# Transposing queries and keys of a head together on all 128 rows, in a fused attention and gated-FFN kernel

## The chip, the core and the metric

The kernel runs on one core of one Trainium2 chip. A core has a matrix engine (TensorE, "PE" in the profile, with its weight loads listed apart as "PEld"), a vector engine (VectorE, DVE), an activation engine (ScalarE, ACT), a general engine (GpSimd, POOL) and a queue engine (SyncE, SP); 16 DMA engines move data between HBM and the on-chip memory. TensorE writes to PSUM banks, which the other engines empty. The metric is the device time of one execution in microseconds (us).

## The reference

The inputs are q, k and v with 8 batches, 12 heads, 448 positions and 64 elements a head, and the three weights of a gated FFN (768 to 1536 and back to 768). Types are float32 outside; the kernel computes in bfloat16 with float32 sums.

```
scores = q k^T / sqrt(64)
attn   = max(scores, 0)^2 / 448
x      = attn v, heads side by side: 3584 rows of 768
out    = (gelu(x w_gate) * (x w_val)) w_out
```

There is no softmax, so no row sums are needed: each block of scores can be activated and squared by itself.

## The kernel before

**Layout.** A batch has 448 = 64 x 7 positions; position p*7 + c lies on partition p in chunk c. `qk16[b]` holds a batch's queries on partitions 0 to 63 and its keys on partitions 64 to 127. All other matmuls are cut into tiles of 64 rows by 64 columns, four of which lie beside each other in the array: two row halves (lists PE0, "lower", and PE1, "upper") and two column halves.

**Stages of a batch.** The scores need q and k with the head dimension on the partitions, so each batch's q and k are first transposed into `qkT`. A pair of heads is the unit: `NPAIR` is 6, and `NM` = 3 groups `m` of two pairs `r` each. For batches 0 and 1 (`EARLY` = 2) TensorE does it (`add_transposes`, the matmuls of line 333) and DVE copies the result out of PSUM (line 339). For later batches `add_dma_transposes` regroups the loaded data on DVE (line 258) and SP issues DMA transposes (line 262). Then come 21 score units a batch (`add_scores`, each with a relu on ScalarE, line 387, and a square on DVE, line 393), the values (`add_values`, copied to `xT` on line 443), gate and value matmuls for 12 blocks `fc` (`add_gate_value`: gelu on line 482, product on line 487), and the output matmuls (`add_out`). Batch b+1's attention runs interleaved with batch b's FFN.

**Transposes before.** For a group the kernel makes 56 matmuls: for both row halves i (0 = q, 1 = k), each pair r, each chunk c and each head j of the pair, a 64x64 block of `qk16` is the stationary operand and the identity moves. Each of the two halves i gathers both pairs in a PSUM area of its own, and its copy writes 64-element pieces into `qkT`. For batch 0 these areas are buffers of `psF` (`FB` = 4, handed out by `new_bank`), for batch 1 the two halves of one buffer of `psS` (`SB` = 2, shared with the scores). Batch 0's first group is handled pair by pair, `rs` = (0,) and then (1,).

**The order.** Nothing is left to a compiler: the schedule is written out by a small planner, `run_plan`. PE0 is a fixed list, sorted by a due time `at` that the loop at the end (lines 610 to 628) gives each step; PE1 follows PE0's positions (`both`: beside it, `then`: after its last). POOL is fixed too, in the order of the load calls on lines 561 to 587. The operations of ACT, DVE, SP and a pseudo-engine IDLE are taken from pools by earliest planned start. An operation is written into the program at the moment it is planned, and each engine executes in that order. `IDLE` operations emit nothing; they stand for the wait on loads ahead of a regrouping copy. Where the plan leaves TensorE idle, `fill` inserts dummy matmuls of `warm` (line 296) as long as the planned time is below `FILL`; `emit_warm_up` (line 676) puts 20 at the start.

**Loads.** POOL issues all loads. q and k of batch 0 come in pieces of heads 0-2, 2-4, 4-8 and 8-12; the FFN's weights follow between batch 1's pieces. Loads of batch b+2 are issued behind products of batch b (lines 500 to 508).

Of the kernel before, what the change touches and what calls it, by code (L numbers as in the profile page):

```python
# [88 lines left out]
def kernel(  # L89
# [10 lines left out]
    nc = tc.nc  # L100
# [6 lines left out]
    P = 64  # L107
# [13 lines left out]
    WOG = 3  # L121
    SB = 2
    FB = 4
    FILL = 64.0
    EARLY = 2

    out_scale = 1.0 / (D * S)
# [110 lines left out]
    def qkT_tile(b):  # L238
        if b not in qkT:
            qkT[b] = tpool.tile([128, NM * SC * 2, 2 * P], bf16, name="qkT", tag="qkT")  # L240
        return qkT[b]

    def by_group(t):
        return t.rearrange("d (m c r) x -> d m c r x", m=NM, c=SC)
# [3 lines left out]
    def add_dma_transposes(b, m):  # L248


        wait = Op("IDLE", 2.0, lambda: None,
                  [head_op[b, pr, i] for pr in (2 * m, 2 * m + 1) for i in range(2)])
        IDLE.append(wait)

        def emit_copy():
            if b not in qkr:
                qkr[b] = lpool.tile([128, NM, SC, 4, D], bf16, name="qkr", tag="qkr")
            nc.vector.tensor_copy(  # L258
                qkr[b][:, m], qk16[b].rearrange("p (h c d) -> p c h d", c=SC, d=D)[:, :, 4 * m:4 * m + 4])

        def emit_transpose(c0, c1):
            nc.sync.dma_start_transpose(
                by_group(qkT_tile(b))[:, m, c0:c1].rearrange("d c r x -> d (c r) x"),
                qkr[b][:, m, c0:c1].rearrange("p c h d -> p (c h d)"))

        copy = Op("DVE", 0.65, emit_copy, [wait, *tr_op.get((b - 1, m), ())], lag=0.15, prio=3)
        DVE.append(copy)
        tr_op[b, m] = [Op("SP", 0.19 * 2 * (c1 - c0), lambda c0=c0, c1=c1: emit_transpose(c0, c1),
                          [copy, last_s.get(b - 2)], lag=4.5) for c0, c1 in ((0, VC), (VC, SC))]
        SP.extend(tr_op[b, m])  # L270
# [9 lines left out]
    def new_bank(reader, shape=(128, 512), dtype=f32):  # L280
        in_bank.append(reader)
        return psF.tile(list(shape), dtype, name="ff", tag="F")

    def fill(t0, t1):

        reader = in_bank[-FB] if len(in_bank) >= FB else None
        if reader is not None:
            if reader.end is None:
                return
            t0 = max(t0, reader.end + 0.2)  # L290
        n = int((t1 - t0 - 0.15) / 0.115)
        if t1 > FILL or n < 1:
            return
        t = new_bank(None)
        for _ in range(n):
            nc.tensor.matmul(t[:, 0:256], warm[:, 0:128], warm[:, 0:256], start=True, stop=True)  # L296

    def ring_dep():
        return [ring[-FB]] if len(ring) >= FB else []
# [19 lines left out]
    def add_transposes(at, b, m, rs):  # L319

        box = {}

        def emit(i, n, c):
            if b and not box:
                t = psS.tile([128, 2, 1024], bf16, name="sp", tag="S")
                for x in range(2):
                    box[x] = t[:, x, 0:len(rs) * SC * P].rearrange("d (r x) -> d r x", r=len(rs))
            elif i not in box:
                box[i] = new_bank(t_op[b, m, rs[0], i], [128, len(rs), SC * P], bf16)
            t = box[i]  # L330
            src = qk16[b].rearrange("p (h c d) -> p h c d", c=SC, d=D)
            for j in range(2):
                nc.tensor.transpose(  # L333
                    t[HALF[j], n, c * P:(c + 1) * P], src[HALF[i], 2 * (2 * m + rs[n]) + j, c, :],
                    ident[HALF[i], HALF[i]], tile_position=(P * i, P * j))

        def emit_copy(i):
            dst = by_group(qkT_tile(b))[:, m].rearrange("d c r x -> d r c x")
            nc.vector.tensor_copy(  # L339
                dst[:, rs[0]:rs[-1] + 1, :, HALF[i]],  # L340
                box[i].rearrange("d r (c p) -> d r c p", c=SC))

        ops = [[], []]
        for i in range(2):
            have = [*(head_op[b, 2 * m + r, i] for r in rs), *(units[-SB:1 - SB] if b else ring_dep())]
            for n in range(len(rs)):
                for c in range(SC):
                    ops[i].append(Op(f"PE{i}", 0.05, lambda i=i, n=n, c=c: emit(i, n, c),
                                     have, lag=0.2))
            t = Op("DVE", 0.07 + 0.235 * len(rs), lambda i=i: emit_copy(i),  # L350
                   [ops[i][-1], last_s.get(b - 2)], lag=0.2, prio=1)
            for r in rs:
                t_op[b, m, r, i] = t
            DVE.append(t)
            if not b:
                ring.append(t)
        if b:
            units.append(t)
        both(at, zip(*ops), GS / 2 if b else 0.0)

    def add_scores(at, b, u):


        m, w = divmod(u, SC)
        tail = w == VC - 1
        prs = (2 * m, 2 * m + 1) if tail else (2 * m + (w > VC - 1),)
        cl = w if w < VC else w - VC
        box = {}

        def emit(j, pr):  # L370
            if not box:
                box[0] = psS.tile([128, 2, 512], f32, name="sp", tag="S")
            sp = box[0]
            t = by_group(qkT_tile(b))[HALF[j], m, :, pr % 2, :]
            for i in range(2):
                if tail:
                    n0 = (pr % 2) * S // 2
                    qs = t[:, :, i * P // 2:(i + 1) * P // 2]
                    mm(sp[HALF[i], j, n0:n0 + S // 2].rearrange("k (c p) -> k c p", c=SC),
                       t[:, VC - 1, HALF[1]], qs, j, i, True, True)  # L380
                else:
                    mm(sp[HALF[i], j, 0:S].rearrange("k (c p) -> k c p", c=SC),
                       t[:, cl + i * VC, HALF[1]], t[:, :, HALF[0]], j, i, True, True)

        def emit_relu():
            rl = box[1] = rpool.tile([128, 2, S], bf16, name="rl", tag="rl")
            nc.scalar.activation(rl[:, :, :], box[0][:, :, 0:S], AF.Relu)  # L387

        def emit_sq():
            a = apool.tile([128, 2, S], bf16, name="attnT", tag="attnT")  # L390
            for pr in prs:
                att[b, pr, VC - 1 if tail else cl] = a
            nc.vector.tensor_tensor(a[:, :, :], box[1][:, :, :], box[1][:, :, :], op=ALU.mult)  # L393

        if b < EARLY:
            have = [t_op[b, m, pr % 2, i] for pr in prs for i in range(2)]
        else:
            have = tr_op[b, m]
        have = [*have, *units[-SB:1 - SB]]
        ops = [[Op(f"PE{j}", 0.095 if tail else 0.189, lambda j=j, pr=pr: emit(j, pr), have, lag=0.24)  # L400
                for pr in prs] for j in range(2)]
        last_s[b] = ops[1][-1]
        relu = Op("ACT", 0.8, emit_relu, [ops[0][-1], ops[1][-1], *sq_list[-4:-3]], lag=0.18, prio=2)
        n_a = len(sq_list)
        sq = Op("DVE", 0.54, emit_sq, [relu, *att_free[n_a - 12:n_a - 11]] if n_a >= 12 else [relu],
                lag=0.2, prio=2)
        units.append(relu)
        sq_list.append(sq)
        att_free.append(None)
        for pr in prs:  # L410
            sq_op.setdefault((b, pr), []).append((sq, n_a))
            sq_of[b, pr, VC - 1 if tail else cl] = sq
        ACT.append(relu)
        DVE.append(sq)
        both(at, zip(*ops))
# [194 lines left out]
    for b in range(B):  # L610
        if b == 0:
            lo, hi = -60.0, -12.0
        elif b == 1:
            lo, hi = LO1, starts[1] - LEAD
        elif b == 2:
            lo, hi = starts[1] + 6.0, starts[2] - LEAD
        else:
            lo, hi = starts[b - 1] - LEAD, starts[b] - LEAD
        step = (hi - lo) / NU
        if b < EARLY:  # L620
            for m in range(NM):
                for rs in ((0,), (1,)) if b == m == 0 else ((0, 1),):
                    work.append((lo + SC * m * step - (5.0 if b else 3.0), 1, add_transposes, (b, m, rs)))
        for pr in range(NPAIR):
            u = SC * (pr // 2) + (VC - 1, SC - 1)[pr % 2]
            work.append((lo + u * step + max(4.5, (3.2 if b == 0 else 2.5) * step), 2, add_values, (b, pr)))
        for u in range(NU):
            work.append((lo + u * step, 3, add_scores, (b, u)))
# [83 lines left out]
```

## Time and profile before

| | us |
|---|---|
| median of 4 runs | 432.11 |
| lowest and highest | 431.10 and 433.21 |
| the profiled execution | 431.10 |
| its span in the profile | 429.3 |

The span runs from the first to the last instruction on the core; 1.8 us of the profiled execution's time lie around it. The second part of the page cuts the span into 40 slices of 10.7 us; each digit is the busy share in tenths.

```
PE   8989799999999999999999999999999999999995
DVE  3966565377544674366623675346633555212200
ACT  3956564276665655555455565555546555222221
DMA  7999999999334895269923798259913100220024
```

Transposes of line 333 fall into the first five slices (5.6 to 53.7 us); the dummy matmuls of line 296 run from 6.1 to 28.6 us. In the profile's groups by line a name such as `qkT<-ff` says what is written from what; `sp` is a buffer of `psS`, `ff` one of `psF`. In a time line the columns are start, length, engine, line, operation, names and count; in brackets stands how long the engine was idle before it and what released it, where "issue" means that the profile shows nothing it waited for.

| group | count | mean ns |
|---|---|---|
| transposes, line 333, matmuls | 336 | 192 to 201 |
| their weight loads | 336 | 112 |
| DVE copy of 896 elements to `qkT`, line 339 | 10 | 620 to 623 |
| DVE copy of 448 elements to `qkT`, line 339 | 4 | 389 |
| regrouping copy, line 258 | 18 | 1080 |
| relu of a score unit, line 387 | 168 | 920 |
| square of a score unit, line 393 | 168 | 623 |

Matmul lengths include their latency; matmuls overlap, so the mean is not what one costs in a row of many.

### The profile page before, as it was taken

Reading aid. Unit: us, or ns where it says so; the run is one execution under the profiler, and the core shown is the slowest. Engines: PE = TensorE matmul, PEld = TensorE weight load, DVE = VectorE, ACT = ScalarE, POOL = GpSimd, SP = SyncE. Lnnn points to the kernel's source line nnn. Section 1 sums busy time; section 2 is a strip of 40 time slices with the busy share of each in tenths; the row PEclk is TensorE's granted clock in tenths of the full one; section 3 lists DMA queues with packets and bytes.
Section 4 is the critical chain, followed back from the end, with each engine's and each line's share of the span. In section 5 each row is a group of like instructions: output and inputs, shape, how many; then the busy total and the mean of one; then the engine's idle time right before and its main releaser. Section 6 shows DMA issues by size and latency. Waiting matters only on the chain.

```text
span 429.3 us, 19964 instructions
## 1 busy us (share of the span) xinstructions
PE 418.5 (97%) x9279; PEld 365.1 (85%) x9279; DVE 212.2 (49%) x345; ACT 224.6 (52%) x323; POOL 71.6 (17%) x117
## 2 busy tenths in 40 slices
PE   8989799999999999999999999999999999999995
PEld 4668599778998888979999978979999978977895
DVE  3966565377544674366623675346633555212200
ACT  3956564276665655555455565555546555222221
POOL 8655420123000230023100230012200000000000
PEclk9999999999999999999999999999999999999998
DMA  7999999999334895269923798259913100220024
GB/s 106 197 199 198 201 208 183 165 148 164 59 76 96 86 173 60 76 105 148 122 52 101 91 157 93 76 81 145 147 40 77 40 4 2 52 64 3 3 76 111
DMA packets 75378, 44.92 MB, mean 105 GB/s; under 512 B 36128, under 2 KB 71840, under 8 KB 75296
## 3 DMA queue, kind: packets, MB, share of 16 engines
q0 software_dynamic: 37088, 24.39, 43.1%
q1 hardware_dynamic: 37968, 19.08, 26.1%
q8 instruction: 72, 1.18, 1.1%
q10 hardware_dynamic: 240, 0.20, 0.2%
q14 instruction: 10, 0.08, 0.1%
HBM read 48.76 MB, written 11.01 MB: 139 GB/s over the span
## 4 chain that ended last, share of the span: by engine, by line
PE 94%; DVE 3%; ACT 1%; issue 1%; ACTq 0%
PE ff L159 84%; PE sp L159 7%; DVE attnT L393 1%; PE ff L676 1%; ACT rl L387 1%; DVE qkT L339 1%; PE ff L296 1%; PE sp L333 1%; DVE xT L443 0%; PE ff L333 0%; ACT osb L538 0%; ACTq L543 0%; DVE warm L145 0%; ACTq L387 0%; ACTq L538 0%
## 5 line engine op out<-in xcount | busy, mean ns | idle before, releaser
L159 PE MATMUL ff<-xT,wg 64*64 64x448 bf16 x2304 | 219.4, 349 | 2.2 <-issue 2.2
L159 PE MATMUL ff<-xT,wv 64*64 64x448 bf16 x2304 | 218.4, 349 | 0.0
L387 ACT ACTIVATE rl<-sp 128x896 bf16<-128x896 f32 x168 | 152.1, 920 | 101.6 <-PE sp L159 81.3
L159 PE MATMUL ff<-wo,uT 64*64 64x384 bf16 (+1 forms) x2736 | 150.7, 320 | 0.5 <-issue 0.5
L159 PEld LDWEIGHTS <-wg 64*64 64x64 bf16 x2304 | 127.1, 107 | 17.4 <-issue 3.5
L393 DVE TENSOR_TENSOR attnT<-rl 128x896 bf16<-128x896 bf16 x168 | 104.0, 623 | 74.9 <-ACT rl L387 73.5
L159 PEld LDWEIGHTS <-wv 64*64 64x64 bf16 x2304 | 127.3, 107 | 14.5 <-issue 1.6
L159 PEld LDWEIGHTS <-uT 64*64 64x64 bf16 x2736 | 126.4, 107 | 5.0 <-issue 0.9
L159 PE MATMUL sp<-qkT 64*64 64x448 bf16 (+1 forms) x768 | 106.8, 327 | 1.1 <-ACT rl L387 0.9
L487 DVE TENSOR_TENSOR uT<-gel,ff 128x448 bf16<-128x448 bf16 x96 | 59.5, 620 | 74.6 <-PE ff L159 64.1
L159 PE MATMUL ff<-attnT,v 64*64 64x448 bf16 (+1 forms) x768 | 85.4, 326 | 0.4 <-DVE attnT L393 0.4
L482 ACT ACTIVATE gel<-ff 128x448 bf16<-128x448 f32 x96 | 52.1, 543 | 49.2 <-PE ff L159 48.0
L538 ACT COPY osb<-ff 128x384 f32<-128x384 f32 (+1 forms) x57 | 26.8, 471 | 50.1 <-PE ff L159 46.9
L159 PEld LDWEIGHTS <-qkT 64*64 64x64 bf16 x768 | 44.0, 106 | 8.3 <-issue 3.3
L159 PEld LDWEIGHTS <-v 64*64 64x64 bf16 x768 | 45.6, 107 | 4.7 <-issue 0.7
L443 DVE TENSOR_SCALAR xT<-ff 128x448 bf16<-128x448 f32 x48 | 29.9, 623 | 32.2 <-PE ff L159 31.5
L211 POOL DMA_DIRECT2D qk<-in_q_dram x25 | 15.5, 622 | 156.2 <-DVE uT L487 147.4
L224 POOL DMA_DIRECT2D v<-in_v_dram x44 | 27.3, 628 | 33.5 <-DVE uT L487 25.4
L211 POOL DMA_DIRECT2D qk<-in_k_dram x25 | 15.4, 615 | 38.9 <-DVE uT L487 27.9
L258 DVE COPY qkr<-qk 128x1792 bf16<-128x1792 bf16 x18 | 19.4, 1080 | 0.9 <-DMA qk<-in_k_dram 0.5
L333 PEld LDWEIGHTS <-qk 64*64 64x64 bf16 x336 | 8.9, 112 | 3.9 <-issue 2.5
L333 PE MATMUL sp<-ident,qk 64*64 64x64 bf16 x168 | 6.2, 192 | 0.9 <-DVE qkT L339 0.8
(22 smaller groups left out, 44.4 us busy)
## 6 DMA issues: line engine op xcount, KB each, us to landing
out_dram<-osb SPq DMA_DIRECT2D x54, 192.0 KB, 2.7
v<-in_v_dram POOLq DMA_DIRECT2D x42, 128.0 KB, 6.2
qk<-in_q_dram POOLq DMA_DIRECT2D x23, 224.0 KB, 4.9
qk<-in_k_dram POOLq DMA_DIRECT2D x23, 224.0 KB, 5.4
wg<-in_moe_w_gate_dram POOLq DMA_DIRECT2D x6, 384.0 KB, 10.5
wv<-in_moe_w_val_dram POOLq DMA_DIRECT2D x6, 384.0 KB, 11.3
wo<-in_moe_w_out_dram POOLq DMA_DIRECT2D x4, 576.0 KB, 14.9
v<-in_v_dram POOLq DMA_DIRECT2D x2, 384.0 KB, 11.9
```

Of the source, the lines that this page charges most:

```text
L159: return nc.tensor.matmul(o, lhsT, rhs, start=start, stop=stop, tile_position=(P * row, P * col))
L211: op = load(4 * (h1 - h0) * S * D, lambda: nc.gpsimd.dma_start(tile_of().rearrange("p (h x) -> p h x", h=H)[:, h0:h1, :], src[b, h0:h1].re ...
L224: return nc.gpsimd.dma_start(v16[b][HALF[i], h0:h1, :, :], v[b, h0:h1].rearrange("h (p c) d -> p h c d", c=SC)[:, :, c0:c0 + VC, :])
L258: nc.vector.tensor_copy(qkr[b][:, m], qk16[b].rearrange("p (h c d) -> p c h d", c=SC, d=D)[:, :, 4 * m:4 * m + 4])
L296: nc.tensor.matmul(t[:, 0:256], warm[:, 0:128], warm[:, 0:256], start=True, stop=True)
L333: nc.tensor.transpose(t[HALF[j], n, c * P:(c + 1) * P], src[HALF[i], 2 * (2 * m + rs[n]) + j, c, :], ident[HALF[i], HALF[i]], tile_positio ...
L387: nc.scalar.activation(rl[:, :, :], box[0][:, :, 0:S], AF.Relu)
L393: nc.vector.tensor_tensor(a[:, :, :], box[1][:, :, :], box[1][:, :, :], op=ALU.mult)
L443: nc.vector.tensor_scalar_mul(xT[b][:, pr, :], box[0][:, 0:S], scalar1=out_scale)
L482: nc.scalar.activation(gel[b, fc][:, :], box[0][:, 0:S], AF.Gelu)
L487: u_op[b, fc].ins = nc.vector.tensor_tensor(uT[b][:, fc, :], gel.pop((b, fc))[:, :], box[0][:, 0:S], op=ALU.mult).ins
L538: nc.scalar.copy(ob[:, cols], box[0][:, 0:N])
```

## The change

- A transpose now takes all 128 rows: the stationary operand is a block of queries and keys of one head (128 rows, 64 columns), the whole 128x128 identity moves, and the result has 64 rows (the head dimension) and 128 columns (64 of q, 64 of k). The two heads j of a pair go to the two column halves. A pair takes 14 such matmuls, a group 28.
- Each pair has one PSUM bank and one DVE copy, of 896 elements in pieces of 128. In batch 1 the two pairs of a group take the two halves of one `psS` buffer.
- In the plan a pair's transposes are one operation `lo` of cost 0.5 on PE0 that emits all 14, with a placeholder `hi` on PE1 that emits nothing.
- Scores of a pair depend on that pair's copy alone.
- In batch 0 the two pairs of every group are placed apart: the first where the group stood, the second 1.5 score units after the group's first score unit's due time. In batch 1 the first group is due 2.0 instead of 5.0 before its scores; the others stay at 5.0.
- From batch 3 on, a regrouping copy is planned 5.0 instead of 2.0 after its loads.
- Dummy matmuls have 512 columns instead of 256, are reckoned at 0.22 instead of 0.115 each, and stop at a planned time of 30 instead of 64.

```diff
--- before.py
+++ after.py
@@ -121,7 +121,7 @@
     WOG = 3
     SB = 2
     FB = 4
-    FILL = 64.0
+    FILL = 30.0
     EARLY = 2
 
     out_scale = 1.0 / (D * S)
@@ -248,7 +248,7 @@
     def add_dma_transposes(b, m):
 
 
-        wait = Op("IDLE", 2.0, lambda: None,
+        wait = Op("IDLE", 2.0 if b == EARLY else 5.0, lambda: None,
                   [head_op[b, pr, i] for pr in (2 * m, 2 * m + 1) for i in range(2)])
         IDLE.append(wait)
 
@@ -288,12 +288,12 @@
             if reader.end is None:
                 return
             t0 = max(t0, reader.end + 0.2)
-        n = int((t1 - t0 - 0.15) / 0.115)
+        n = int((t1 - t0 - 0.15) / 0.22)
         if t1 > FILL or n < 1:
             return
         t = new_bank(None)
         for _ in range(n):
-            nc.tensor.matmul(t[:, 0:256], warm[:, 0:128], warm[:, 0:256], start=True, stop=True)
+            nc.tensor.matmul(t[:, :], warm[:, 0:128], warm[:, :], start=True, stop=True)
 
     def ring_dep():
         return [ring[-FB]] if len(ring) >= FB else []
@@ -320,43 +320,37 @@
 
         box = {}
 
-        def emit(i, n, c):
-            if b and not box:
-                t = psS.tile([128, 2, 1024], bf16, name="sp", tag="S")
-                for x in range(2):
-                    box[x] = t[:, x, 0:len(rs) * SC * P].rearrange("d (r x) -> d r x", r=len(rs))
-            elif i not in box:
-                box[i] = new_bank(t_op[b, m, rs[0], i], [128, len(rs), SC * P], bf16)
-            t = box[i]
+        def emit(r):
+            if b == 0:
+                t = new_bank(t_op[b, m, r], [128, SC, 2 * P], bf16)
+            else:
+                if not box:
+                    box["S"] = psS.tile([128, 2, 1024], bf16, name="sp", tag="S")
+                t = box["S"][:, r, 0:SC * 2 * P].rearrange("d (c x) -> d c x", c=SC)
+            box[r] = t
             src = qk16[b].rearrange("p (h c d) -> p h c d", c=SC, d=D)
-            for j in range(2):
-                nc.tensor.transpose(
-                    t[HALF[j], n, c * P:(c + 1) * P], src[HALF[i], 2 * (2 * m + rs[n]) + j, c, :],
-                    ident[HALF[i], HALF[i]], tile_position=(P * i, P * j))
-
-        def emit_copy(i):
-            dst = by_group(qkT_tile(b))[:, m].rearrange("d c r x -> d r c x")
-            nc.vector.tensor_copy(
-                dst[:, rs[0]:rs[-1] + 1, :, HALF[i]],
-                box[i].rearrange("d r (c p) -> d r c p", c=SC))
-
-        ops = [[], []]
-        for i in range(2):
-            have = [*(head_op[b, 2 * m + r, i] for r in rs), *(units[-SB:1 - SB] if b else ring_dep())]
-            for n in range(len(rs)):
-                for c in range(SC):
-                    ops[i].append(Op(f"PE{i}", 0.05, lambda i=i, n=n, c=c: emit(i, n, c),
-                                     have, lag=0.2))
-            t = Op("DVE", 0.07 + 0.235 * len(rs), lambda i=i: emit_copy(i),
-                   [ops[i][-1], last_s.get(b - 2)], lag=0.2, prio=1)
-            for r in rs:
-                t_op[b, m, r, i] = t
+            for c in range(SC):
+                for j in range(2):
+                    nc.tensor.transpose(t[HALF[j], c, :], src[:, 2 * (2 * m + r) + j, c, :],
+                                        ident[:, :], tile_position=(0, P * j))
+
+        def emit_copy(r):
+            nc.vector.tensor_copy(by_group(qkT_tile(b))[:, m, :, r, :], box[r])
+
+        last = units[-SB:1 - SB]
+        for r in rs:
+            have = [*(head_op[b, 2 * m + r, i] for i in range(2)), *(last if b else ring_dep())]
+            lo = Op("PE0", 0.5, lambda r=r: emit(r), have, lag=0.2)
+            hi = Op("PE1", 0.4, lambda: None)
+            hi.after = lo
+            t = t_op[b, m, r] = Op("DVE", 0.54, lambda r=r: emit_copy(r),
+                                   [lo, last_s.get(b - 2)], lag=0.2, prio=1)
             DVE.append(t)
             if not b:
                 ring.append(t)
+            both(at, [(lo, hi)])
         if b:
             units.append(t)
-        both(at, zip(*ops), GS / 2 if b else 0.0)
 
     def add_scores(at, b, u):
 
@@ -393,7 +387,7 @@
             nc.vector.tensor_tensor(a[:, :, :], box[1][:, :, :], box[1][:, :, :], op=ALU.mult)
 
         if b < EARLY:
-            have = [t_op[b, m, pr % 2, i] for pr in prs for i in range(2)]
+            have = [t_op[b, m, pr % 2] for pr in prs]
         else:
             have = tr_op[b, m]
         have = [*have, *units[-SB:1 - SB]]
@@ -619,8 +613,10 @@
         step = (hi - lo) / NU
         if b < EARLY:
             for m in range(NM):
-                for rs in ((0,), (1,)) if b == m == 0 else ((0, 1),):
-                    work.append((lo + SC * m * step - (5.0 if b else 3.0), 1, add_transposes, (b, m, rs)))
+                for rs in ((0,), (1,)) if b == 0 else ((0, 1),):
+
+                    x = (1.5 * step if rs == (1,) else -3.0) if b == 0 else -5.0 if m else -2.0
+                    work.append((lo + SC * m * step + x, 1, add_transposes, (b, m, rs)))
         for pr in range(NPAIR):
             u = SC * (pr // 2) + (VC - 1, SC - 1)[pr % 2]
             work.append((lo + u * step + max(4.5, (3.2 if b == 0 else 2.5) * step), 2, add_values, (b, pr)))
```

## The prediction

> **What bounds the kernel now.** I read the page's first part and its chain, then the time line of the first 80 us (the only stretch in which TensorE transposes run), then counts by window.
>
> ```profile
> span 429.3 us, 19964 instructions
> PE 418.5 (97%) x9279; PEld 365.1 (85%) x9279; DVE 212.2 (49%) x345; ACT 224.6 (52%) x323; POOL 71.6 (17%) x117
> PE 94%; DVE 3%; ACT 1%; issue 1%; ACTq 0%
> q8 instruction: 72, 1.18, 1.1%
> ```
>
> TensorE holds 94% of the chain, nearly all of it matmuls that the change leaves alone. From about 80 us to the end there is nothing to win or lose except a constant shift. What can move lies in three early stretches.
>
> *Batch 0 attention, 8 to 26 us*, is paced by ScalarE, 0.83 us a unit, with one hole:
>
> ```profile
> 7.94 11.62 ACT L387 ACTIVATE rl<-sp 128x896 bf16<-128x896 f32 x14 [5.70 <-PE sp L159]
> 19.95 5.78 ACT L387 ACTIVATE rl<-sp 128x896 bf16<-128x896 f32 x7 [0.39 <-PE sp L159]
> 30.93 0.92 ACT L387 ACTIVATE rl<-sp 128x896 bf16<-128x896 f32 x1 [5.21 <-PE sp L159]
> ```
>
> *The hand-over, 26 to 30 us*: the last values, batch 1's first transposes and the first gate matmuls mix, and ScalarE idles 5.21 us. *Batch 1 beside batch 0's FFN, 30 to 76 us*: here TensorE should be full and is not.
>
> ```profile
> 38.18 0.22 PE L333 MATMUL sp<-ident,qk 64*64 64x64 bf16 x2 [0.41 <-DVE qkT L339]
> 52.26 0.38 PE L159 MATMUL ff<-xT,wg 64*64 64x448 bf16 x2 [1.94 <-issue]
> 53.66 0.22 PE L333 MATMUL sp<-ident,qk 64*64 64x64 bf16 x2 [0.39 <-DVE qkT L339]
> 76.50 0.84 PE L159 MATMUL ff<-wo,uT 64*64 64x384 bf16 x16 [0.54 <-issue]
> ```
>
> Two waits of 0.4 us are for DVE's copy of the transposes. The two "issue" holes have no releaser; windows cut at them explain them (after the length: PE, PEld, DVE, ACT, POOL busy with counts, granted clock, DMA share, GB/s):
>
> ```profile
> 39.86:46.06 6.20, 6.20 (x130) 5.11 (x128) 4.01 (x8) 4.32 (x6) 2.70 (x4) 1.00 1.45 197
> 46.06:52.26 6.20, 4.27 (x130) 3.37 (x128) 2.85 (x5) 2.81 (x4) 3.02 (x5) 1.00 1.41 202
> 52.26:76.49 24.23, 23.31 (x512) 21.25 (x512) 15.00 (x24) 12.41 (x17) 3.33 (x5) 1.00 1.25 190
> 76.49:106.75 30.26, 30.00 (x640) 24.96 (x640) 18.29 (x29) 17.70 (x25) 7.33 (x12) 1.00 1.30 164
> ```
>
> From hole to hole TensorE issued about 258, then 258, then exactly 1024 and 1280 instructions: multiples of 256. The instruction queue q8 carried 72 packets, 1.18 MB, so 16.4 KB each, and 18,558 TensorE instructions over 72 is 258. TensorE runs out of instructions at packet boundaries while the DMA engines are loaded (DMA share over 1.2). From 39.86 to 76.49 that is 6 packets in 36.63 us: 6.1 us for 256. Plain FFN work needs less: between 40 and 45 us 112 matmuls and 112 loads took 5.00 us, so 5.7 us for 256. The packet with the third group of transposes was eaten in 4.27 us and then starved for 1.94.
>
> *A rule against the row.* The Trainium skill (Runtime: NRT & Kernel Launch, Instruction fetch mechanics) says that code comes in 16 KiB blocks of 256 instructions and that crossing a block is "mostly hidden". The block size agrees with this trace; the hiding does not hold here. By the rule, halving the transposes saves no fetch time; by the row, each group's 56 fewer instructions are worth up to 56/256 x 6.1 = 1.3 us. I take the row, through the walk below.
>
> **The change, part by part.**
>
> *Transposes.* 336 transposes of 64x64 with as many weight loads become 168 of 128x64 (q and k together), each moving 128 columns of the identity. No row shows this form, so from both sides. Nearest rows: the fills on line 296 in the time line, all 128 rows:
>
> ```profile
> 6.13 1.24 PE L296 MATMUL ff<-warm 128*128 128x256 bf16 x5
> 8.03 0.61 PE L296 MATMUL ff<-warm 128*128 128x256 bf16 x4
> ```
>
> and, in the groups by shape (busy us, mean ns), the warm-up and the old transposes:
>
> ```profile
> L676 PE MATMUL ff<-warm 128*64 128x512 bf16 x20 | 4.5, 634 | 1.2 <-DVE warm L145 1.2
> L333 PE MATMUL sp<-ident,qk 64*64 64x64 bf16 x168 | 6.2, 192 | 0.9 <-DVE qkT L339 0.8
> ```
>
> At 8.03 a fill of 256 columns costs (0.61-0.28)/3 = 0.11 us (0.28 is a lone one), its weight load hidden; so 128 columns cost 0.055. At 6.13 it is (1.24-0.42)/4 = 0.21: half speed, though the granted clock reads 1.00 there. The warm-up (line 676) put 20 matmuls of 512 columns through in 4.48 us at that half speed, 0.42 each if alone, so the two column halves ran side by side. A group of 28 is then 14 x 0.055 = 0.77 us. Upper bound: no side-by-side and loads exposed, about 0.17 a pair (0.055 plus a load of 0.11), 2.3 us. I take 0.77, because load hiding and pairing are both seen.
>
> *A rule that speaks against the change.* TensorEngine Tiling (Array Packing), Key Properties: changing the tiling mode drains TensorE. The old transposes shared the 64x64 mode with all their neighbours; the new ones switch twice a group. The row: scores starting at 12.20 stream for 0.19, a fill starts at 12.49, streams 0.11, and the values start at 12.70: 0.10 each way. A full drain by the rule would be a matmul's latency beyond its stream, 0.35-0.19 = 0.16 each way. Per group 0.2 by the row, 0.32 by the rule; I take 0.2, and 0.1 more because the two row halves stand out of phase. New group: 1.1 us. The old one: in 35.16 to 38.20 us stand 105 matmuls, 49 of them not transposes, worth 49 x 5.00/112 = 2.2 us; of the other 0.84, 0.41 is the wait, so some 0.4 to 0.6 with refilling. So 1.1 against 1.0 with its wait: alone, no gain.
>
> *The copies' wait goes.* It arose because the first half's copy stood in the program ahead of the other half's last transposes in the same PSUM tile. Now a group's two operations follow each other at once and both copies come behind: 0.41 + 0.39 = 0.8 us off (counted in the 1.0). If it stays, the groups cost 0.8 more. DVE copies: 620 ns before and after (896 elements); only the four of 389 ns become two of 620, -0.3 us on an engine half idle.
>
> *Fetch, a walk from 35.1 us.* TensorE index boundaries shift by some 260 until then (four groups with 56 fewer each, some 19 fills fewer at two each), nearly one packet, so the phase is about the old one. Packet 1 (56 transpose instructions, 200 others): 200/44.8 + 1.1 = 5.6 to 5.8, ending near 40.85. Then 256 plain at the 6.1 pace: 47.0. Then the third group's packet: work 5.8, pace 6.1: 53.2, at a point the old kernel reached near 55.3. Four more packets at the larger of 5.7 and 6.1 lead to 77.7 at the point that stood at 79.0. Gain 1.3 us. Bounds: 0 if the starving merely moves to another packet, 2.7 (112/256 x 6.1) if all of it counts. The fourth hole near 106.7 (0.6 us) falls elsewhere: -0.3, an even chance.
>
> *Start.* Scores sat at 7.31 behind the second group's transposes, whose k load, issued at 3.70, needs 3.6 us (the first: 1.98 to 5.60). That group moves 1.5 units later, so this wait goes. But at half speed 7 pairs take 0.75 + 0.2 instead of 0.59, one copy 0.62 instead of two of 0.69 together, and fills of 512 columns are coarser: scores near 7.5. +0.2 us (-0.1 to +0.6).
>
> *Batch 0's hole of 0.39* came from the third group's copies at 17.15 and 18.81, both needed before any score. Now only the first pair's is: -0.3 (-0.4 to 0). If gone, the next limit is ScalarE's own 0.83.
>
> *Hand-over.* Batch 1's first group moves from 3.0 ahead of the first gate matmul to directly ahead of it: no longer among the values but between their row halves. The last xT copy (28.72 now) waits for upper values behind two blocks of 0.6: later by 0.7, less 0.1 to 0.2 for a wait on the copy that went. +0.5 (-0.3 to +1.2). Everything queued on TensorE behind it moves along.
>
> *Regroup wait 2.0 to 5.0 from batch 3 on.* 15 copies (1.08 us) and their 30 DMA transposes on SP's queue stand later, past attnT, uT and xT work on DVE and output stores on SP. Waits recorded before these copies sum to 0.9 us on DVE, not TensorE's path. The consumer, the next batch's scores, comes some 21 units later. 0 (-0.5 to 0); POOL's loads keep their order.
>
> *Fills.* The last old fill ran at 28.63, so the limit 30 instead of 64 takes nothing away; widths double, counts halve, which is time that waited anyway: 0.
>
> **Sum.** +0.2 - 0.3 + 0.5 - 1.3 - 0.3 = -1.2 us: the profiled execution's 431.1 (span 429.3 and 1.8 around it) becomes 429.9. That execution is the quickest of the four; on their median, 432.11, it gives 430.9. A measurement of this kernel can tell about 0.5%, 2.16 us, from no change, so this is "same".
>
> **Rivals.**
> *Starving goes for good.* Fewer instructions take 2.7 us off between 35 and 76 us, the 0.6 near 106 goes, and the hand-over costs 0.2: -2.7-0.6-0.3+0.2+0.2 = -3.2, so 428.9. For it: holes at exact multiples. Against: plain FFN work at 5.7 leaves only 0.4 a packet.
> *Full-array transposes serialise.* If load and move don't overlap or the halves don't pair, batch 1's three groups cost 2.3 + 0.3 instead of 1.1: +1.5 each, 4.5 in all; with -1.2 that is +3.3: 435.4. It costs more than my other terms win from 1.5 us a group on (3 x 0.4 = 1.2) and can be told from 2.2 on. Against: the fills and warm-up rows.
> *The change doesn't act.* The fetch hole merely moves and the hand-over eats the rest: +0.1, 432.2; still "same".
>
> **How the numbers follow.** My forecast with its own range 429.5 to 433.5: 0.42; not acting: 0.12; starving gone: 0.31; serialised: 0.15. Faster 0.32, same 0.53, slower 0.15. The range 428.3 to 434.3 takes in the fast rival and leaves out most of the serialised one.
>
> **What would show it.** Right: transposes in blocks of 14 within about 0.6 us; no wait of line 333 on DVE; the hole near 52 us below 0.5; the first relu near 8.1; ScalarE without a hole at 19.5. Wrong: blocks over 0.9 us; a new hole over 1 us at another multiple of 256; gate matmuls resuming later than 30.5 us.

## The result, and the profile after

The changed kernel took 431.57 us (median of 43 runs, 430.02 to 434.57) against 432.68 us (median of 64 runs, 429.96 to 437.68) for the kernel before, measured beside it. The ratio is 0.9981, with a 95% interval of 0.9969 to 0.9993: a gain of 0.2%, small but outside chance. Forecast were 430.9 us and a ratio of 0.997. The size came out nearly right, but by luck: a term put at nothing carries much of the gain, and the others miss in both directions. The rest of this document is about that. One execution of e5_regroup2 (438.26 us) was in the chip's slow state and is left out of its median below.

The profiled execution of the changed kernel took 431.43 us. These are the lines of its page that answer to those of before (span; busy time of each engine; shares of the chain that ended last; the instruction queue with packets, MB and share):

```profile
span 429.5 us, 19597 instructions
...
PE 421.2 (98%) x9094; PEld 357.1 (83%) x9094; DVE 211.2 (49%) x343; ACT 225.0 (52%) x323; POOL 71.6 (17%) x117
...
q8 instruction: 71, 1.16, 1.1%
...
PE 93%; DMA 2%; DVE 2%; ACT 1%; issue 1%; POOL 1%; ACTq 0%; POOLq 0%
```

367 instructions and one packet of code have gone, and the span is 0.2 us *longer* than in the profile of before (429.3). So the two profiled executions show no gain at all. That of before took 431.10 us, which is 1.6 us under its kernel's median of 64 runs; that of after stands at its kernel's median. A pair of single profiles that differs by less than the spread of the runs can't show where the gain is; further profiles of both kernels were needed.

**Where the time goes in the pair.** ScalarE's relus, in the time line of after (start, length, ..., idle time before it and its releaser):

```profile
7.00 1.73 ACT L381 ACTIVATE rl<-sp 128x896 bf16<-128x896 f32 x2 [4.77 <-PE sp L159]
9.35 3.47 ACT L381 ACTIVATE rl<-sp 128x896 bf16<-128x896 f32 x4 [0.62 <-PE sp L159]
13.29 0.92 ACT L381 ACTIVATE rl<-sp 128x896 bf16<-128x896 f32 x1 [0.47 <-PE sp L159]
14.57 5.02 ACT L381 ACTIVATE rl<-sp 128x896 bf16<-128x896 f32 x6 [0.36 <-PE sp L159]
19.97 6.89 ACT L381 ACTIVATE rl<-sp 128x896 bf16<-128x896 f32 x8 [0.38 <-PE ff L159]
33.24 0.92 ACT L381 ACTIVATE rl<-sp 128x896 bf16<-128x896 f32 x1 [6.38 <-PE sp L159]
```

The first relu comes 0.9 us earlier than before (7.00, was 7.94), and then four holes of 0.62, 0.47, 0.36 and 0.38 follow where there was one. The waits of TensorE in the first 60 us name the first two (in total, times, longest):

```profile
PE ff L334 <- DMA qk<-in_k_dram: 1.4, 2, 0.9
...
PE sp L159 <- DVE qkT L338: 0.2, 1, 0.2
PE ff L159 <- DVE xT L437: 0.2, 1, 0.2
```

The first group's second pair and, behind it, the first pair of the second group each waited among the scores for a piece of k. The two pieces landed at 7.94 and 12.21 us here and at 6.94 and 10.71 in the profile of before. By the 19th relu the changed kernel is 1.2 us behind.

The hand-over, in TensorE's time line of after, and below it the first value matmul of the FFN in that of before:

```profile
27.98 0.58 PE L334 MATMUL sp<-ident,qk 128*64 128x128 bf16 x14
28.49 0.38 PE L159 MATMUL ff<-attnT,v 64*64 64x448 bf16 x2
28.80 0.58 PE L334 MATMUL sp<-ident,qk 128*64 128x128 bf16 x14
29.31 0.38 PE L159 MATMUL ff<-attnT,v 64*64 64x448 bf16 x2
...
31.69 0.38 PE L159 MATMUL ff<-xT,wg 64*64 64x448 bf16 x2 [0.15 <-DVE xT L437]
31.88 0.57 PE L159 MATMUL ff<-xT,wv 64*64 64x448 bf16 x4
```

```profile
29.57 0.57 PE L159 MATMUL ff<-xT,wv 64*64 64x448 bf16 x4
```

From the start of the 19th relu (24.33, before 23.15) to the first value matmul of the FFN pass 7.55 us, before 6.42: 1.1 more, and 2.3 us behind in all. Nearly all of this comes back at 52 us, where the old hole was. The third group of batch 1 there:

```profile
50.72 0.35 PE L159 MATMUL ff<-xT,wv 64*64 64x448 bf16 x2
51.00 0.58 PE L334 MATMUL sp<-ident,qk 128*64 128x128 bf16 x14
51.51 0.38 PE L159 MATMUL ff<-attnT,v 64*64 64x448 bf16 x2
51.82 0.58 PE L334 MATMUL sp<-ident,qk 128*64 128x128 bf16 x14
52.33 0.38 PE L159 MATMUL ff<-xT,wg 64*64 64x448 bf16 x2
```

No wait for a copy stands here and no hole behind it; the kernel is 0.3 us behind at 57 us, where it was 2.2 at 43.6. From 107 us on, where a second old hole of 0.6 is missing, it is 0.1 behind, and 0.2 at the end. Losses and gains of the first 107 us cancel, in this pair.

### The profile page after: what moved, and what is told of

Read it like the earlier page. It is cut to its first block, busy times and chain, and to the rows that moved or that the text cites. A ratio compares the mean times of both kernels' runs of the same rounds, so it can differ in the third digit from the quotient of the medians.

```text
span 429.5 us, 19597 instructions
## 1 busy us (share of the span) xinstructions
PE 421.2 (98%) x9094; PEld 357.1 (83%) x9094; DVE 211.2 (49%) x343; ACT 225.0 (52%) x323; POOL 71.6 (17%) x117
## 4 chain that ended last, share of the span: by engine, by line
PE 93%; DMA 2%; DVE 2%; ACT 1%; issue 1%; POOL 1%; ACTq 0%; POOLq 0%
PE ff L159 85%; PE sp L159 7%; DMA qk<-in_k_dram 2%; ACT rl L381 1%; PE sp L334 1%; DVE attnT L387 1%; POOL qk L211 1%; DVE xT L437 1%; DVE qkT L338 0%; ACT osb L532 0%; PE ff L334 0%; ACTq L537 0%; PE ff L296 0%; POOL ident masks.py:199 0%; POOL ident masks.py:197 0%
## 5 line engine op out<-in xcount | busy, mean ns | idle before, releaser
L159 PE MATMUL ff<-xT,wg 64*64 64x448 bf16 x2304 | 218.8, 349 | 0.2 <-DVE xT L437 0.2
L159 PE MATMUL ff<-xT,wv 64*64 64x448 bf16 x2304 | 217.8, 349 | 0.4 <-issue 0.2
L159 PE MATMUL ff<-wo,uT 64*64 64x384 bf16 (+1 forms) x2736 | 150.8, 320 | 0.0
L159 PEld LDWEIGHTS <-wv 64*64 64x64 bf16 x2304 | 126.2, 107 | 17.7 <-issue 3.0
L159 PEld LDWEIGHTS <-wg 64*64 64x64 bf16 x2304 | 125.9, 107 | 17.5 <-issue 1.3
L159 PEld LDWEIGHTS <-uT 64*64 64x64 bf16 x2736 | 125.0, 107 | 5.7 <-issue 0.4
L159 PE MATMUL sp<-qkT 64*64 64x448 bf16 (+1 forms) x768 | 108.1, 328 | 0.3 <-DVE qkT L338 0.2
L159 PE MATMUL ff<-attnT,v 64*64 64x448 bf16 (+1 forms) x768 | 85.9, 327 | 0.1
L532 ACT COPY osb<-ff 128x384 f32<-128x384 f32 (+1 forms) x57 | 26.8, 471 | 49.8 <-PE ff L159 46.6
L159 PEld LDWEIGHTS <-qkT 64*64 64x64 bf16 x768 | 43.2, 106 | 10.4 <-issue 4.0
L159 PEld LDWEIGHTS <-v 64*64 64x64 bf16 x768 | 45.0, 107 | 6.0 <-issue 1.2
L334 PEld LDWEIGHTS <-qk 128*64 128x64 bf16 x168 | 5.1, 109 | 4.4 <-issue 4.4
L338 DVE COPY qkT<-ff 128x896 bf16<-128x896 bf16 x6 | 3.7, 623 | 7.7 <-PE ff L334 7.7
```

The source lines that it names most:

```text
L159: return nc.tensor.matmul(o, lhsT, rhs, start=start, stop=stop, tile_position=(P * row, P * col))
L334: nc.tensor.transpose(t[HALF[j], c, :], src[:, 2 * (2 * m + r) + j, c, :], ident[:, :], tile_position=(0, P * j))
L338: nc.vector.tensor_copy(by_group(qkT_tile(b))[:, m, :, r, :], box[r])
L532: nc.scalar.copy(ob[:, cols], box[0][:, 0:N])
```

## The experiments

The theory to be tested: the first 107 us cancel on the whole, and the gain of the medians comes from the regrouping copies, which in most executions of the kernel before hold up work that the profiled one shows hardly. The rivals: that the gain is the missing code (56 instructions fewer in each group), with the copies worth nothing; and that placement in batch 0 or at the hand-over decides. An expectation names its theories by letters of its own.

### Does the instruction count set the pace of batch 1? (e3_pad)

In the changed kernel, every score matmul of batch 1 is followed by one of 16 columns that writes spare columns of the same bank, which nobody reads: 96 tiny matmuls with 96 weight loads, hardly any work.

```diff
+            if b == 1:
+                mm(sp[HALF[i], j, S:S + 16], warm[HALF[j], 0:P], warm[HALF[j], 0:16], j, i, True, True)
```

> The changed kernel with 96 more tiny matmuls of 16 columns and their weight loads beside batch 1's scores (192 TensorE instructions, some 1.2 us of array time at the 12.5 ns a piece of the old transposes; their results are not used). Theory A (batch 1's stretch is paced by instruction packets): 192/256 of a packet at 6.1 us, up to 4.6 us longer, at least 3, with issue holes of over 1 us at multiples of 256. Theory B (array time alone): at most 1.2 us longer than the changed kernel, no new holes.

433.69 us (ratio 1.0016, 1.0000 to 1.0033), 2.4 us above e1_hand in the same series. This is between the two expectations and nearer to the count. The waits from 40 to 80 us:

```profile
PE ff L159 <- issue: 1.6, 4, 0.5
PE ff L159 <- DVE xT L439: 0.6, 1, 0.6
```

Counting TensorE's instructions in the trace, distances of 0.67, 0.95, 0.59, 0.72 and 0.87 us between two starts of matmuls (0.19 is usual) end at instructions 1474, 1730, 1986, 2242 and 2498, at 47.0, 53.2, 59.2, 65.1 and 71.3 us: five boundaries of 256 in a row, one packet every 5.9 to 6.2 us. At the second of them the profile names a copy to `xT`, which ended 0.3 us before, so that hole may have either cause, and not all of the 2.4 us need be fetching.

The times of queue q8's packets in the trace say the same of the others. At each of these boundaries TensorE went on 1.3 to 1.6 us after the packet had landed; the packet had set out 3.6 to 3.8 us after the boundary before, and took 0.9 to 1.0. These three add to about 6.1 us, and a TensorE that gets through a packet sooner waits. In the changed kernel's profile the same 1.3 to 1.7 us stand at every boundary from 43 to 79 us: it runs at the pace of its code there without showing a hole.

### Placement (e1_hand, e2_together)

e1_hand puts batch 1's first group back to 5.0 before its scores; e2_together puts both pairs of each later group of batch 0 where the group stood.

```diff
-                    x = (1.5 * step if rs == (1,) else -3.0) if b == 0 else -5.0 if m else -2.0
+                    x = (1.5 * step if rs == (1,) else -3.0) if b == 0 else -5.0
```

> The changed kernel with one thing undone: batch 1's first group of transposes is due 5.0 before its scores again, not 2.0. Theory A (two thirds of the 2.3 us that the changed kernel is late at the first full gate matmul come from the hand-over, one from holes in batch 0's relus): gate matmuls resume about 1.2 us earlier (near 30.5 instead of 31.7 us), and about 430.5 us in time, 0.5% under the kernel before. Theory B (the lateness comes from late loads and batch 0's holes alone): resume within 0.3 us of 31.7 less what the holes change, time as the changed kernel's 431.6.

The trace shows the program of the changed kernel again: the other engines' instructions stand in the same order, and from the 19th relu to the first value matmul pass the same 7.55 us. The loop at the end of the kernel says why. The last pair's values are due at -7.0 and the first gate matmul at 0; the group is due at -3.0 with the one edit and at 0 with the other, and nothing else is due between. So this edit of the change does nothing, and the run is a second look at the changed kernel: 431.28 us (22 runs, ratio 0.9965, 0.9947 to 0.9983). Its own value is another hole, in TensorE's time line:

```profile
77.80 0.35 PE L159 MATMUL ff<-xT,wg 64*64 64x448 bf16 x2
80.68 0.38 PE L159 MATMUL ff<-xT,wv 64*64 64x448 bf16 x2 [2.53 <-issue]
```

It stands at instruction 2754, a boundary of 256. In the profile of after, the same instruction came 0.41 us after the one before (78.86 to 79.27), in e2_together 1.5. So the changed kernel has a starving place too, at 79 us, where two starts lay 0.4 us apart in one execution and 2.9 in the other. In these three profiles the code packet there took 1.2 to 3.8 us to arrive, against 0.9 to 1.0 at the boundaries before, while batch 2's DMA transposes (72 to 84 us) used the DMA engines.

```diff
-                for rs in ((0,), (1,)) if b == 0 else ((0, 1),):
+                for rs in ((0,), (1,)) if b == m == 0 else ((0, 1),):
-                    x = (1.5 * step if rs == (1,) else -3.0) if b == 0 else -5.0 if m else -2.0
+                    x = (-3.0) if b == 0 else -5.0 if m else -2.0
```

> The changed kernel with both pairs of batch 0's second and third group placed together again, as before. Theory A (holes in batch 0's relus come from the second pair's separate block, which splits scores and values and waits for loads in the middle): one or two of the four holes (0.62, 0.47, 0.36, 0.38 us) go, the 21st relu ends 0.5 to 0.8 us earlier than 26.9 us. Theory B (the holes come from loads that landed late in that one execution): the holes stay or go with the landing of the k loads, whatever the placement.

431.55 us (ratio 0.9967, 0.9948 to 0.9986), the same as e1_hand. The first relu starts at 8.50 instead of 7.00 us, there is no wait for k, and the 21st relu ends at 27.14 instead of 26.86. In these two executions, placing the pairs apart wins 1.5 us at the start and loses it to late loads and to the transposes among the scores.

### The kernel before, seen again (e4_before_again, e11_before_third)

Both are the kernel before, without an edit, for a second and third profile.

> The kernel before once more, for a second profile. Theory A: the 1.9 us hole stands at the same TensorE instruction (0.2 us either way in length), the DVE waits of 0.4 us too. Theory B (holes are an accident of that execution): they stand elsewhere or not at all.

434.7 us. The hole at 52 us is there again, of the same length (2.29 us between two starts) and at the same instruction, 1986. New is this, in DVE's time line

```profile
94.62 1.09 DVE L258 COPY qkr<-qk 128x1792 bf16<-128x1792 bf16 x1 [1.98 <-DMA qkT<-qkr]
95.63 0.61 DVE L487 TENSOR_TENSOR uT<-gel,ff 128x448 bf16<-128x448 bf16 x1
```

and beside it in TensorE's:

```profile
94.64 0.35 PE L159 MATMUL ff<-xT,wv 64*64 64x448 bf16 x2
96.29 0.38 PE L159 MATMUL ff<-xT,wv 64*64 64x448 bf16 x4 [1.29 <-DVE uT L487]
```

A regrouping copy stood first in DVE's order and waited 2 us for DMA transposes still reading its buffer. The product behind it (line 487) empties a PSUM buffer, and the next value matmul waited 1.29 us for that. In the whole execution TensorE waited 1.6 us for such products; in the profile that the prediction read, not once.

> The kernel before, a third profile. Theory A of the regrouping wait: a wait of over 0.5 us of a regrouping copy on DVE for a load or a DMA transpose in some batch, and gate matmuls that wait for a product behind it. The hole of 2.29 us at the 1986th instruction once more.

434.06 us. A copy waited 1.3 us for the DMA transposes and others 0.9 for k; TensorE waited 0.7 for a product. The hole at instruction 1986 stood there a third time, and two more of about 1.0 us between two starts at 108 and 316 us, both at boundaries of 256.

### The regroup wait alone, both ways (e5_regroup2, e6_before5, e12_regroup2_again)

e6_before5 is the kernel before with the later regrouping, and nothing else of the change; e5_regroup2 is the changed kernel without it, and e12_regroup2_again the same for another profile.

```diff
-        wait = Op("IDLE", 2.0, lambda: None,
+        wait = Op("IDLE", 2.0 if b == EARLY else 5.0, lambda: None,
```

> The kernel before with only the regrouping copies planned 5.0 after their loads. Theory A: some 1 us faster than before, the whole gain of the change. Theory B: no difference from before; the hole of 2.29 us at the 1986th TensorE instruction stands in both cases.

431.95 us, ratio 0.9983 (0.9964 to 1.0002): the whole change's 0.9981, from this edit alone. TensorE's waits in its profile begin so:

```profile
PE ff L159 <- issue: 2.2, 2, 1.9
```

The hole at 52 us is still there (2.29 us at instruction 1986, the fourth time), yet the time is that of the changed kernel. No copy of line 258 waits for a load, and no matmul for a product.

> The changed kernel with the regrouping copies planned 2.0 after their loads again. Theory A (the longer wait is worth something in ordinary executions, because a copy that stands too early on DVE waits for a late load and products and the gate matmuls behind it wait too; the profile of before was an execution without it): about 1 us slower than the changed kernel, 432.4, with DVE waits for loads or DMA transposes before the copies. Theory B (my forecast: the copies' place costs nothing, the gain is in the instruction packets of batch 1): 431.4, no difference from the changed kernel.

433.48 us (13 runs, 430.63 to 435.55), ratio 1.0014 (0.9985 to 1.0042): the changed kernel without the later regrouping shows no gain. The copies waited 2.4 us for k, in five places. Yet its longest idle time on TensorE is of the other kind:

```profile
264.61 0.33 PE L159 MATMUL ff<-wo,uT 64*64 64x384 bf16 x2
267.37 0.35 PE L159 MATMUL ff<-wo,uT 64*64 64x384 bf16 x2 [2.42 <-issue]
```

This is instruction 10943, at the end of a packet of code; the next packet began to arrive at 264.5 us, 5.5 us after the boundary before, where it took 2.5 in the profile of after. The copy before it ran at 255.23, its DMA transposes from 256.3 to 260.3: nobody waited for them here.

> The changed kernel with the 2.0 wait, a second profile. Theory A (copies stand and hold products up): DVE waits of over 1 us in all before the copies and TensorE waits on products. Theory C (the earlier DMA transposes slow the fetch of instruction packets down): issue holes of over 0.5 us in batches 2 to 6 within 10 us behind a regrouping copy, and no TensorE wait on products.

432.31 us in one execution. The stall of the copies shows. DVE:

```profile
256.23 1.09 DVE L258 COPY qkr<-qk 128x1792 bf16<-128x1792 bf16 x1 [1.91 <-DMA qk<-in_k_dram]
257.23 0.61 DVE L387 TENSOR_TENSOR attnT<-rl 128x896 bf16<-128x896 bf16 x1
257.76 0.61 DVE L481 TENSOR_TENSOR uT<-gel,ff 128x448 bf16<-128x448 bf16 x1
```

TensorE:

```profile
256.81 0.39 PE L159 MATMUL ff<-xT,wg 64*64 64x448 bf16 x4
258.43 0.38 PE L159 MATMUL ff<-attnT,v 64*64 64x448 bf16 x2 [1.23 <-DVE uT L481]
```

The copy waited 1.91 us for its k, the square and the product queued behind it, and the next matmul 1.23 us for the product. Of the five profiles with the wait of 2.0, three (e4, e11, e12) have it, and its longest wait is 0.7 to 1.3 us; of the nine with 5.0 only e3_pad has a copy that waits (0.5 us) and a wait for a product (0.5 us).

All fourteen profiles can be asked at once. From the 800th of the FFN's matmuls (near 80 us) to the last of them pass 344.7 (the profile of before), 345.8, 346.9, 347.0 and 347.3 us with the wait of 2.0, and 344.3 to 345.1 us in the nine with 5.0. The averages are 346.3 and 344.8. Four of the five lie above all nine; the fifth is the execution that the prediction read.

The mechanism is shown. The size is less sharp: 1.5 us by these averages; 0.7 us by the ratio of e6_before5, whose interval just reaches nothing; 1.9 us between the medians of e5_regroup2 and the changed kernel, and 1.4 by their two ratios, whose intervals overlap. Whether the long hole of e5_regroup2 has to do with the earlier copies or is the chance of a packet stays open.

### The hand-over (e7_early10)

Batch 1's first group of the changed kernel is due 10.0 before its scores, which puts it ahead of the last pair's values.

```diff
-                    x = (1.5 * step if rs == (1,) else -3.0) if b == 0 else -5.0 if m else -2.0
+                    x = (1.5 * step if rs == (1,) else -3.0) if b == 0 else -5.0 if m else -10.0
```

> The changed kernel with batch 1's first group of transposes due 10.0 before its scores, which puts it ahead of the last pair's values instead of between their row halves. Theory A (the hand-over's 1.1 us are the two blocks of transposes ahead of the last values' upper half): gate matmuls resume in full 0.8 to 1.3 us earlier relative to the 19th relu (6.4 us behind it as before, not 7.5), 430.4. Theory B (the hand-over is set by the switch of the array's mode and the copies wherever the group stands): 7.5 us behind it, no gain.

The group is now due at -8.0, before the -7.0 of the last pair's values. 429.96 us (16 runs), ratio 0.9919 (0.9895 to 0.9943). TensorE's time line and ScalarE's:

```profile
25.12 0.97 PE L334 MATMUL sp<-ident,qk 128*64 128x128 bf16 x28
26.02 0.86 PE L159 MATMUL ff<-attnT,v 64*64 64x224 bf16 x16
...
29.09 0.54 PE L159 MATMUL ff<-xT,wv 64*64 64x448 bf16 x4
```

```profile
18.83 6.89 ACT L381 ACTIVATE rl<-sp 128x896 bf16<-128x896 f32 x8 [0.38 <-PE ff L159]
30.43 0.92 ACT L381 ACTIVATE rl<-sp 128x896 bf16<-128x896 f32 x1 [4.71 <-PE sp L159]
```

All 28 transposes run in a row, in 0.9 us, while TensorE still waits for the last squares, and the values of both row halves then follow undivided. From the 19th relu to the first value matmul of the FFN pass 5.90 us, against 7.55: 1.65 us won, and the medians differ by 1.6. (Its profile had no late k at the start either: its first value matmul stands 2.8 us ahead of that of after, and its span is 2.1 us shorter.)

### Dummy matmuls and the place of the packets (e8_fills256, e9_warm48, e10_best)

e8_fills256 gives the changed kernel its old dummies back: 256 columns, reckoned at 0.115, until 64. That adds 48 TensorE instructions. e9_warm48 adds 48 as well, but in the warm-up of the start (44 matmuls of 232 columns instead of 20 of 512), and leaves the other dummies at 512 columns. The two diffs:

```diff
-    FILL = 30.0
+    FILL = 64.0
...
-        n = int((t1 - t0 - 0.15) / 0.22)
+        n = int((t1 - t0 - 0.15) / 0.115)
...
-            nc.tensor.matmul(t[:, :], warm[:, 0:128], warm[:, :], start=True, stop=True)
+            nc.tensor.matmul(t[:, 0:256], warm[:, 0:128], warm[:, 0:256], start=True, stop=True)
```

```diff
-        for _ in range(10):
+        for _ in range(22):
...
-                nc.tensor.matmul(t[HALF[j], :], warm[:, HALF[j]], warm[:, :],
+                nc.tensor.matmul(t[HALF[j], 0:232], warm[:, HALF[j]], warm[:, 0:232],
```

> The changed kernel with the dummy matmuls of before (256 columns, limit 64). My forecast's step: no difference from the changed kernel within 0.3 us, since they fill time that waits; some 48 instructions more shift the packet boundaries by 48 instructions and move the holes without changing their sum by over 0.5 us. Rival (finer dummies end sooner, so that real work starts sooner): up to 0.5 us faster.

430.07 us, ratio 0.9948 (0.9926 to 0.9970).

> The changed kernel with the warm-up cut finer: 44 dummy matmuls of 232 columns in the place of 20 of 512, the same array time and 48 TensorE instructions more, so that the packet boundaries fall where they fall with the finer dummies of e8_fills256. Theory A (those dummies gain 1.5 us because the boundaries move off the batch 2 DMA transposes at 79 us): about 430.1, the hole at 79 us under 0.6. Theory B (finer dummies let real work start sooner): no gain, 431.4, the hole at 79 us as variable as in the changed kernel (0.4 to 2.9).

430.35 us, ratio 0.9950 (0.9924 to 0.9975): the same 1.2 to 1.5 us under the changed kernel, with its dummies unchanged. So it is not that finer dummies leave less behind them. In both profiles the code now crosses a packet elsewhere in the same work: at instruction 2754, now at 76 us, two starts lie 0.42 us apart in e8_fills256 and 0.31 in e9_warm48, against 0.4 and 2.9 in the two profiles of the changed program. The place of the gain can be read too. From the first value matmul of the FFN to the 800th FFN matmul pass 47.2 to 47.7 us in the three profiles with 48 instructions more (e10_best below is one), and 48.3 to 49.8 in the six with the changed kernel's count (after, e1_hand, e2_together, e5_regroup2, e7_early10, e12_regroup2_again). On average that is 1.4 us, the whole of it.

e10_best has the edits of e7_early10 and e8_fills256 together.

> Both winning edits together: batch 1's first group ahead of the last values, dummies of 256 columns. If their gains of 1.6 and 1.5 us add: 428.5, ratio to before 0.989. If the second was only a matter of where packet boundaries fall, and the first moves them in time again: 429 to 430, as e7_early10 alone.

429.56 us (8 runs), ratio 0.9926 (0.9900 to 0.9952). The two gains don't add; its profile has 1.8 us of waits for late k at the start, and 0.77 us between two starts at instruction 2754. Why the second edit brings so little here was not taken further. Both e7_early10 and e10_best beat the kernel before and the changed one.

## Why the prediction was right or wrong

**The step that failed is the regroup wait**, costed at "0 (-0.5 to 0)" because "Waits recorded before these copies sum to 0.9 us on DVE, not TensorE's path". With it fell "From about 80 us to the end there is nothing to win or lose except a constant shift". It measured -0.7 us (e6_before5) to -1.9 us (e5_regroup2 against the changed kernel), and alone it gives the ratio of the whole change. The reading was true of the execution that was read, but that was the quickest of the four shown, by 1 us against their median, and it had none of the waits for products that two later executions of the same kernel had (1.6 and 0.7 us). The sum was moved to the median by adding a constant 1 us, as if what a quick execution lacks could not be touched by the edit. Reading what is queued behind a waiting copy (a product, and behind it a PSUM buffer that TensorE needs) would have given it a price.

**The sum was right by luck.** Take the four profiles with the old transposes, and for each part six that share the changed kernel's. On average the new transposes lose 0.5 us up to the 19th relu (-0.1 forecast) and 1.1 at the hand-over (+0.5), and win 1.8 from there to 80 us (-1.3). Behind 80 us the profiles with later copies win 1.5 (0, and -0.3 for a packet). These are averages of single executions and come to -1.7 us, where the medians say -1.1. Without the later copies little is left: e5_regroup2 stands at 1.0014 (0.9985 to 1.0042), which is the rival in which the change doesn't act (+0.1).

**Fetching** was understood: -1.3 forecast at 52 us, 2.0 won back there, and the hole never seen again in that place. But the step took the new phase "about the old one" and let every later packet run at the larger of work and pace. In fact the starving came up at 79 us, where the plan had none, with 0.4 to 2.9 us between two starts: the sign of a "new hole over 1 us at another multiple of 256" that had been named, in e1_hand and e2_together. That the other terms eat this gain is seen in e6_before5, which keeps the old hole and is as fast. The even chance of -0.3 near 107 us came true: that hole is gone.

**The hand-over** was mis-sized: +0.5 forecast, +1.1 measured, and gates resumed in full at 31.69 us, beyond the 30.5 set as a sign of error; 1.2 us of that is lateness from before the hand-over. The mechanism was right: two blocks stand ahead of the last pair's upper values, and e7_early10 wins the time back by moving them. The reason given for their place, the later due time, was wrong: that edit changes nothing (e1_hand). From the first block's start to the second's end, at 27.98 and 29.31, are 1.33 us, less 0.19 for the two value matmuls between: 1.1, where 0.7 was reckoned and 0.1 to 0.2 taken off for the copies.

**The transposes** cost what was worked out. The matmuls at 50.72 stream until 50.91; from there to 52.33 are 1.42 us, less 0.19 for the two matmuls between the blocks: 1.23 us a group, against 1.1. From 50.91 to 51.00 are 0.09 us, and a block's 0.51 leaves 0.12 beside 7 x 0.055. Read as the two changes of mode, they came nearer to the row's 0.10 than to the 0.16 of a drain. As a group is two blocks, it has four changes and not two. The copies' wait is gone, as said. The rival in which the blocks serialise (2.6 us a group) is refuted.

**Start and batch 0's hole** had the wrong signs: first relu at 7.00 and not 8.1, since the second pair's transposes left the way of the first scores, as forecast, and a block took 0.58 us, not 0.95; and a hole of 0.38 stands at 19.97 again, which the profile lets end on values placed ahead of scores ("PE ff L159") and not on the third group's copies. Together they end at +1.2 us in this execution, mostly by late pieces of k, which other executions of both kernels have or lack (0 to 1.8 us in the profiles). The first relu itself starts at 7.1 to 7.9 us in the four profiles with the old transposes and at 6.9 to 7.9 in the six, so the 0.9 us of the pair is mostly the chance of two executions.

**Dummies** at 0: true as work, but 48 instructions more move the packets and are worth 1.2 to 1.5 us (e8_fills256, e9_warm48). No row of the profile of before could give that number.

## What to carry to other kernels

Before a wait is costed at nothing, look at what its engine does behind it, and at the profiled execution's place among the runs: a quick one can lack the very stalls that an edit removes. Where transposes or other blocks become undivided, check where the first block stands against the last work that a hand-over waits for; an earlier place was worth 1.6 us here. And where TensorE idles at multiples of a packet of code, a few instructions more or fewer elsewhere can be worth more than the edit under study, so compare with a run that only shifts the code.

## What had not been expected of the hardware

- A hole of 2.29 us came at the same instruction (1986) in all four profiles of programs with the old transposes, to within 0.01 us: starving for code is not noise there. The length is the distance between two starts, of which 1.94 us are idle. At instruction 2754 of the changed program this distance was 0.41 us in one execution and 2.88 in the other.
- Between 40 and 72 us of e3_pad a packet of 256 instructions came every 5.9 to 6.2 us, although many of its instructions did hardly any work: some 3.7 us until it set out, 0.9 on the way, 1.4 until TensorE went on. The packet's transfer is the least of it; what the first 3.7 us wait for is not shown.
- Transposes of 128 rows in pairs of column halves cost 0.064 us a pair in the row of 28 of e7_early10 (0.90 us for 14 pairs, its ends included). Their 28 weight loads, recorded at 0.11 us each, are hidden in that.
